# Attention and a SoLU layer on one core: low weight bits and lower halves moved to GpSimd, sums of squares to TensorE, larger units, another order

## The chip, the cores and the metric

The kernel runs on one core of one Trainium2 chip. A core has five engines that this kernel uses, each with a queue that it works through strictly in order: TensorE (PE: matrix products out of SBUF into PSUM), VectorE (DVE), ScalarE (ACT), GpSimd (POOL) and SyncE (SP), which only issues DMA transfers. Engines wait for each other by semaphores. The metric is the device time of one execution in microseconds (us).

## The reference

Attention with masks in 8 batches and 8 heads, then a SoLU layer (a product, a gate by softmax, a normalisation, a product). Cut to what is computed:

```python
# q, k, v: (8, 8, 576, 64) float32; w_in (512, 1024), w_out (1024, 512), g_ln (1024): float64
scores = np.matmul(q, k.transpose(0, 1, 3, 2)) / np.sqrt(64)
mask_local = (rel >= 0) & (rel < 32)                              # heads 0 to 3
mask_strided = (rel >= 0) & (pos[None, :] % 32 == pos[:, None] % 32)   # heads 4 to 7
attn = softmax(np.where(masks, scores, -1e9))
x = np.matmul(attn, v).transpose(0, 2, 1, 3).reshape(4608, 512)

h = x @ w_in
sm = softmax(h)
solu = h * sm
ln = (solu - mean(solu)) / np.sqrt(var(solu) + 1e-06) * g_ln
return (ln @ w_out).astype(np.float32)
```

## The kernel before, in words

**Plan and order.** The program is first written down as numbered steps: `add(engine, duration, function, reads, writes)`. A table of some 1,500 step numbers, `ORDER`, then says in which order the steps are issued, and with that the order in every engine's queue. The durations play no part in the order once the table is there. The semaphores follow from what each step reads and writes. So who stands behind whom is set by the table alone.

**Attention, in units.** Each batch has five units (`UNITS`): two for the strided heads (6 and 5 blocks of 54 queries) and three for the local heads (3 blocks each of 64 queries against 96 keys). One unit goes: score products of `q` and `k` into `s_ps` (L374), onto a mask seed that was written there before (for the first units by TensorE with a unit matrix, L369, from then on by ScalarE, L361); maximum of each row on VectorE (L380) and subtraction (L390) or, for some local units, the exponential block by block on ScalarE (L385); exponential (L392), row sum (L393), reciprocal (L397, L398), multiplication by it on GpSimd (L401); split of the probabilities into an upper half in float16 (ScalarE, L409) and a lower half (VectorE, L410); a transposing DMA (L412); product with `v` into `x_ps` (L432 strided, L442 local); split of `x` into halves (L461 ScalarE, L462 VectorE). `v` is scaled by a power of two that comes from the sum of its squares (L303 on ScalarE, L264, L270 and following) and split likewise (L325, L326).

**The SoLU layer, in 36 tiles of 128 tokens.** As soon as a batch's x is there, its tiles follow. FF1 (L505 to L507) is 24 products of 128x512: for each chunk upper by upper, upper by lower, lower by upper half. Then maximum (L511), exponential (ScalarE, L515), product with the exponential (VectorE, L517), mean and variance (L521, L522), some ten tiny steps on GpSimd (L525 to L555, for the first tiles L532 to L541), split of the normalised tile `cc` (L562 ScalarE, L563 VectorE), transposing DMA (L566), FF2 with `w_out` (L575 to L577, 24 products), output (L583).

**The weights.** They arrive as 64-bit numbers, 4 MB each in four pieces of 1 MB (`load`, L285, into `raw`, the last but one piece of w_out into `cc`). ScalarE makes a float32 of the upper word (`decode`, L603), VectorE shifts the lower word down (L606) and ORs three more bits in (L607). Then a power of two is found for a whole matrix from the sum of its squares: for w_in by TensorE (products of each block with itself, L620, of which VectorE reads the diagonal, L624), for w_out by ScalarE (L639, eight squares with an accumulator, joined with g squared on VectorE, L644 and L645). Then the matrix is split: w_in at L628 and L629, w_out, multiplied by g and the scale (`gs`, L649), at L651 (upper half, ScalarE) and L652 (lower half, VectorE). In the source:

```python
nc.vector.tensor_scalar(w0, w0, 29, None, op0=ALU.logical_shift_right)                       # L606
nc.vector.scalar_tensor_tensor(di, di, 3, w0, op0=ALU.logical_shift_left, op1=ALU.bitwise_or)  # L607
...
nc.vector.scalar_tensor_tensor(olo[:, cc], obuf[:, cc], gs_sb[:, cc : cc + 1], ohi[:, cc], op0=ALU.mult, op1=ALU.subtract)  # L652
```

Of the kernel before, what the change touches and what calls it, by code (L numbers as in the profile page):

```python
# [753 lines left out]
```

## Time and profile before

| what | value |
|---|---|
| three runs | 500.56, 502.09, 501.76 us (median 501.76) |
| profiled execution | 501.38 us, of it 499.7 us span from the first to the last instruction |
| mean granted TensorE clock | 0.952 |
| TensorE, products | 462.6 us busy (93% of the span) |
| VectorE / ScalarE / GpSimd | 352.0 / 363.3 / 159.8 us (70%, 73%, 32%) |
| DMA | 88.03 MB, mean 176 GB/s |

Line numbers (L505) are lines of the kernel before; names such as `h_ps<-w,xl` give output and inputs of an instruction. A bracket behind a row of the timeline, `[0.61 <-DVE raw L517]`, says how long the engine stood idle before it and what ended the wait. A matmul's 0.38 us contains its way through the pipeline; the next one starts earlier.

### The profile page before, as it was taken

The numbers are of one execution on the slowest core, as the hardware profiler recorded it, in microseconds if no ns is written. First come the engines' busy times: TensorE is split into PE (matmuls) and PEld (weight loads), VectorE is DVE, ScalarE is ACT, GpSimd is POOL, SyncE is SP. The second block draws the span as 40 slices with busy tenths as digits, with TensorE's granted clock in tenths as the row PEclk, the third lists the DMA queues.
The fourth block names the chain that finished last, engine by engine and source line by source line (L and its number), as shares of the span: only waits on it lengthen the run. The fifth ranks groups of instructions, "written<-read, shape, count | busy, mean of one in ns | idle before, by whom it ended". The sixth has DMA issues, their size and how long they took to land.

```text
span 499.7 us, 12461 instructions
## 1 busy us (share of the span) xinstructions
PE 462.6 (93%) x5049; PEld 241.4 (48%) x5049; DVE 352.0 (70%) x740; ACT 363.3 (73%) x647; POOL 159.8 (32%) x312
## 2 busy tenths in 40 slices
...
GB/s 330 336 326 261 353 187 163 158 189 184 187 207 180 133 259 257 131 173 231 213 145 197 254 185 175 84 90 218 85 138 121 78 123 101 132 102 74 84 97 106
DMA packets 153818, 88.03 MB, mean 176 GB/s; under 512 B 139808, under 2 KB 140448, under 8 KB 153248
## 3 DMA queue, kind: packets, MB, share of 16 engines
...
q8 instruction: 39, 0.64, 0.5%
q14 instruction: 19, 0.16, 0.1%
...
## 4 chain that ended last, share of the span: by engine, by line
PE 80%; DMA 13%; ACT 3%; SPq 2%; DVE 1%; issue 1%; ACTq 0%; DVEq 0%
PE h_ps L505 11%; PE o_ps L575 11%; PE h_ps L507 11%; PE h_ps L506 11%; PE o_ps L576 11%; PE o_ps L577 11%; PE s_ps L374 6%; DMA raw<-w_in 4%; DMA cc<-cc 3%; DMA raw<-w_out 3%; PE x_ps L442 3%; DMA pt<-p 3%; PE x_ps L432 2%; DMA q<-qstr 1%; ACT t L385 1%
## 5 line engine op out<-in xcount | busy, mean ns | idle before, releaser
L575 PE MATMUL o_ps<-ohi,cc 128*128 128x512 f16 x272 | 103.3, 380 | 0.2
L577 PE MATMUL o_ps<-ohi,cc 128*128 128x512 f16 x272 | 103.1, 379 | 0.0
L576 PE MATMUL o_ps<-obuf,cc 128*128 128x512 f16 x272 | 103.1, 379 | 0.0
L401 POOL TENSOR_TENSOR t<-t,m 128x576 f32<-128x576 f32 (+2 forms) x40 | 48.5, 1214 | 117.3 <-DVE m L398 93.8
L511 DVE TENSOR_REDUCE st<-h_ps 128x1 f32<-128x512 f32 x70 | 47.3, 681 | 32.6 <-PE h_ps L507 32.3
L563 DVE SCALAR_TENSOR_TENSOR cc<-raw,st,cc 128x1024 f16<-128x1024 f32 (+1 forms) x38 | 46.6, 1229 | 23.5 <-ACT cc L562 23.1
L515 ACT ACTIVATE raw<-h_ps,st,vsc 128x512 f32<-128x512 f32 x62 | 47.8, 773 | 19.7 <-DVE st L513 18.8
L505 PE MATMUL h_ps<-w,xl 128*128 128x512 f16 x140 | 53.7, 384 | 1.8 <-DVE raw L517 1.8
L517 DVE SCALAR_TENSOR_TENSOR raw<-h_ps,raw 128x512 f32<-128x512 f32 x70 | 47.1, 683 | 11.7 <-ACT raw L515 11.2
L374 PE MATMUL s_ps<-k,q 64*54 64x54 f32 (+1 forms) x1280 | 45.6, 284 | 9.1 <-ACT s_ps L361 7.4
L507 PE MATMUL h_ps<-w,xl 128*128 128x512 f16 x140 | 53.6, 383 | 0.0
L506 PE MATMUL h_ps<-w,xl 128*128 128x512 f16 x140 | 53.6, 383 | 0.0
L505 PE MATMUL h_ps<-w,xs 128*128 128x512 f16 x140 | 53.5, 382 | 0.0
L521 ACT ACTIVATE raw<-raw,st 128x1024 f32<-128x1024 f32 x36 | 41.3, 1147 | 16.8 <-DVE st L520 15.8
L506 PE MATMUL h_ps<-w,xs 128*128 128x512 f16 x140 | 53.3, 381 | 0.0
L507 PE MATMUL h_ps<-w,xs 128*128 128x512 f16 x140 | 53.3, 381 | 0.0
L562 ACT ACTIVATE cc<-raw,st 128x1024 f16<-128x1024 f32 (+1 forms) x38 | 41.5, 1100 | 13.9 <-POOL st L552 9.6
L374 PEld LDWEIGHTS s_ps<-k,q 64*54 64x54 f32 (+1 forms) x1280 | 40.0, 201 | 19.8 <-ACT s_ps L361 8.8
L380 DVE TENSOR_REDUCE m<-s_ps 128x6 f32<-128x576 f32 (+2 forms) x40 | 30.4, 760 | 25.7 <-PE s_ps L374 25.2
L577 PEld LDWEIGHTS <-cc 128*128 128x128 f16 x288 | 28.2, 98 | 34.5 <-DMA cc<-cc 0.6
L575 PEld LDWEIGHTS <-cc 128*128 128x128 f16 x288 | 28.1, 98 | 33.4 <-DMA cc<-cc 1.0
L576 PEld LDWEIGHTS <-cc 128*128 128x128 f16 x288 | 28.2, 98 | 31.5
...
## 6 DMA issues: line engine op xcount, KB each, us to landing
...
```

What stands on the lines that cost most here:

```text
L374: nc.tensor.matmul(s_ps[row : row + nq, pair, i * nk : (i + 1) * nk], q_raw[half][hs, q0 : q0 + (nq - 1) * nqb + 1 : nqb], k_raw[half][hs, ...
L401: add("pool", nx * nk / 520 + 0.03, lambda: nc.gpsimd.tensor_tensor(tv, tv, sm.unsqueeze(2).broadcast_to([P, nx, nk]), op=ALU.mult), r=TM, ...
L505: nc.tensor.matmul(hv[i], xhi[cc], whi[:, cc, cols], start=(cc == 0), stop=False)
L506: nc.tensor.matmul(hv[i], xhi[cc], wlo[:, cc, cols], start=False, stop=False)
L507: nc.tensor.matmul(hv[i], xlo[cc], whi[:, cc, cols], start=False, stop=(cc == 3))
L511: add("dve", 0.69, lambda i=i: nc.vector.tensor_reduce((nm, nm2)[i], hv[i], axis=AX.X, op=ALU.max, negate=True), r=[HH[i]], w=[(ST, "nm", i)])
L515: add("act", 0.73, lambda i=i, q=q: nc.scalar.activation(e[:, parts2[i]], hv[i], AF.Exp, bias=nm, scale=hs, accum_out=q), r=[HH[i], (ST, " ...
L517: add("dve", 0.7, lambda i=i, x=x: nc.vector.scalar_tensor_tensor(u[:, parts2[i]], hv[i], 1.0, e[:, parts2[i]], op0=ALU.mult, op1=ALU.mult ...
L563: add("dve", w / 980 + 0.23, lambda cols=cols: nc.vector.scalar_tensor_tensor(c[:, 1, cols], u[:, cols], r, c[:, 0, cols], op0=ALU.mult, o ...
L575: nc.tensor.matmul(o, ct[:, cc, :], ohi[:, cc, :], start=(cc == 0), stop=False)
L576: nc.tensor.matmul(o, ct[:, cc, :], olo[:, cc, :], start=False, stop=False)
L577: nc.tensor.matmul(o, ct[:, 8 + cc, :], ohi[:, cc, :], start=False, stop=(cc == 7))
```

## The change

1. *Units.* From batch 1 on the local heads go in units of 5 and 4 blocks (`LATER`) instead of three of 3; batch 0 keeps its five. The buffers `t`, `p` and `pt` have sizes of their own per kind of unit (four `p` buffers, three before). A unit of five blocks uses both banks of `x_ps`.
2. *Low bits.* The shift of the low word (L606 on VectorE) becomes one instruction on GpSimd that reads the top byte of the low word (L618 after). The OR on VectorE waits for it.
3. *Squares of w_out.* ScalarE's eight squares (L639) become 32 products on TensorE (L655 after) and one diagonal on VectorE (L659 after); the sum of the squares of g is multiplied in.
4. *Squares of v*, batches 0 and 1: ScalarE's squares (L303) become 22 products a batch (L310 after) and a diagonal (L313 after).
5. *Lower halves of w_out.* VectorE's one instruction (L652) becomes two on GpSimd, a multiplication (L667 after) and a subtraction (L668 after), eight times.
6. *Seeds.* All mask seeds are written by ScalarE; TensorE's seed products are gone. The opening products of TensorE are 12 of 128x480 instead of 40 of 128x128.
7. *Order.* `ORDER` is a new table. The loads begin with v and the first piece of w_in, then q and k.

What the new order does at three places. First VectorE round the first FF1, whose maximum is L511 (before) and L521 (after); `obuf` is w_out as it is decoded, `m` and `t` are a unit's maxima and scores. Before:

```order
L393 TENSOR_REDUCE m_89<-t_86 128x12
L397 TENSOR_SCALAR m_89<-m_89 128x12
L398 RECIPROCAL m_89<-m_89 128x12
L380 TENSOR_REDUCE m_90<-s_ps 128x10
L462 TENSOR_TENSOR xl_100<-x_ps,xl_99 128x2x192
L390 TENSOR_TENSOR t_87<-s_ps,m_90 128x540
L410 TENSOR_TENSOR p_95<-t_85,p_95 128x6x96
L606 TENSOR_SCALAR cc_103<-cc_103 128x1024
L607 SCALAR_TENSOR_TENSOR obuf_114<-obuf_114,cc_103 128x1024
L511 TENSOR_REDUCE st_106<-h_ps 128x1
L606 TENSOR_SCALAR raw_67<-raw_67 128x1024
```

After, up to the same maximum:

```order
L391 TENSOR_REDUCE m_88<-s_ps 128x10
L401 TENSOR_TENSOR t_84<-s_ps,m_88 128x540
L619 SCALAR_TENSOR_TENSOR obuf_113<-obuf_113,raw_67 128x1024
L640 SCALAR_TENSOR_TENSOR w_112<-cc_102,w_sc_114,w_112 128x1024
L421 TENSOR_TENSOR p_94<-t_85,p_94 128x6x96
L472 TENSOR_TENSOR xl_99<-x_ps,xl_98 128x2x192
L404 TENSOR_REDUCE m_87<-t_83 128x12
L391 TENSOR_REDUCE m_89<-s_ps 128x10
L619 SCALAR_TENSOR_TENSOR obuf_113<-obuf_113,cc_102 128x1024
L404 TENSOR_REDUCE m_88<-t_84 128x10
L398 TENSOR_SCALAR m_89<-m_89 128x10
L521 TENSOR_REDUCE st_105<-h_ps 128x1
```

The shifts (L606) are gone from between; the score blocks of batch 1 (`t_84<-s_ps`, `m_89<-s_ps`) stand ahead of the row sum of the unit before them (L404, before L393).

Second, GpSimd between the units of batch 1 and the small steps of the first tiles (`st_106` before and `st_105` after are tile 0). Before:

```order
L401 TENSOR_TENSOR t_86<-t_86,m_89 128x648
L401 TENSOR_TENSOR t_87<-t_87,m_90 128x540
L532 TENSOR_SCALAR st_106<-st_106 128x1
L533 TENSOR_TENSOR st_106<-st_106,nhalf_111 128x1
L401 TENSOR_TENSOR t_88<-t_88,m_91 128x576
L532 TENSOR_SCALAR st_107<-st_107 128x1
L533 TENSOR_TENSOR st_107<-st_107,nhalf_111 128x1
L525 TENSOR_SCALAR st_106<-st_106 128x1
```

After, in the same stretch:

```order
L412 TENSOR_TENSOR t_84<-t_84,m_88 128x540
L412 TENSOR_TENSOR t_85<-t_85,m_89 128x960
L667 TENSOR_SCALAR obuf_113<-obuf_113,gs_118 128x512
L668 TENSOR_TENSOR obuf_113<-obuf_113,ohi_109 128x512
L542 TENSOR_SCALAR st_105<-st_105 128x1
L543 TENSOR_TENSOR st_105<-st_105,nhalf_110 128x1
```

and, six more pairs of L667 and L668 further on:

```order
L667 TENSOR_SCALAR obuf_113<-obuf_113,gs_118 128x512
L668 TENSOR_TENSOR obuf_113<-obuf_113,ohi_109 128x512
L542 TENSOR_SCALAR st_106<-st_106 128x1
L543 TENSOR_TENSOR st_106<-st_106,nhalf_110 128x1
L535 TENSOR_SCALAR st_105<-st_105 128x1
L536 TENSOR_SCALAR st_105<-st_105,vsc_76 128x1
L537 TENSOR_SCALAR st_105<-st_105 128x1
```

Eight pairs now stand between the products of batch 1's units and the small steps of tile 1 (`st_106`), and one pair ahead of tile 0's.

Third, SyncE's loads round the second to fourth piece of w_out. Before:

```order
L285 DMA raw_67<-w_out 128x2x1024
L661 DMA g_118<-g 128x8
L412 DMA_TRANSPOSE pt_97<-p_96 128x12x128
L285 DMA cc_103<-w_out 128x2x1024
L285 DMA k_65<-kloc 128x1152
L285 DMA raw_67<-w_out 128x2x1024
L285 DMA q_63<-qloc 128x1152
L285 DMA vrs_70<-vstr 128x1536
```

After:

```order
L288 DMA raw_67<-w_out 128x2x1024
L288 DMA q_63<-qloc 128x1152
L288 DMA cc_102<-w_out 128x2x1024
L288 DMA raw_67<-w_out 128x2x1024
L288 DMA vrs_69<-vstr 128x1536
L423 DMA_TRANSPOSE pt_96<-p_94 128x12x128
L288 DMA raw_67<-vstr 128x1536
L288 DMA k_66<-kstr 128x1188
```

Batch 1's local q is now loaded behind w_out's second piece instead of the fourth, and the transposes of `p` stand elsewhere among the loads.

The diff, cut to its core (the whole table is new; two of its lines stand for it):

```diff
+LATER = [(1, 0, 6), (1, 6, 5), (0, 0, 5), (0, 5, 4)]
...
-1 5 7 2 0 6 8 11 10 13 12 15 14 17 9 21 3 25 4 29 53 45 54 55 68 56 46 57 69 47 58 70 59 48 71 49 88 60 72 83 73 61 51 74 89 62 90 84 18 91 52 22 100
+1 5 3 8 16 6 15 11 7 20 9 13 14 25 35 2 30 18 52 17 53 21 22 54 10 55 4 61 12 56 57 59 23 62 60 24 26 27 63 124 64 93 28 77 65 78 94 36 79 125 31 32
...
 def warm(n, out):
-    for _ in range(40):
-        nc.tensor.matmul(o_ps[:, 0:P], ones, ones, start=True, stop=True)
+    for i in range(n):
+        nc.tensor.matmul(out[i % len(out)], ones, ones[:, 0:1].broadcast_to([P, 5 * KL]), start=True, stop=True)
...
 def v_scale(b):
-            def square(a=a):
-                nc.scalar.activation(junk[:, 0 : VW[a]], vr_sb[raw][a], AF.Square, scale=2.0**-SQ, accum_out=vm[:, a : a + 1])
-            add("act", (1.36, 1.58)[a], square, r=[("vr", a, raw)], w=["junk", ("vm", b % 2, a)])
+        if b < 2:
+            for a in (1, 0):
+
+                def gram(a=a):
+                    x = vr_sb[raw][a].bitcast(BF16).rearrange("p (f t) -> p f t", t=2)[:, :, 1]
+                    for i in range(VW[a] // P):
+                        nc.tensor.matmul(h_ps[2][:, 0:P], x[:, i * P : i * P + P], x[:, i * P : i * P + P], start=(a == 1 and i == 0), stop=(a == 0 and i == VW[0] // P - 1))
+
+                add("pe", (0.75, 0.9)[a], gram, r=[("vr", a, raw)], w=[("h", 2)])
+            add("dve", 0.3, lambda: nc.vector.scalar_tensor_tensor(diag, h_ps[2][:, 0:P], 1.0, unit_sb, op0=ALU.mult, op1=ALU.mult, accum_out=vm[:, 0:1]),
+                r=[("h", 2), "unit"], w=[("vm", b % 2, a) for a in range(2)])
...
 def unit(n):
-    half, b0, nb = UNITS[j]
+    half, b0, nb = (LATER if b else UNITS)[j]
...
-        if n >= SEEDED:
-
-            def seed():
-                nc.scalar.copy(s_ps[:, :, 0 : nb * nk], mk.unsqueeze(1).broadcast_to([P, 2, nb * nk]))
-
-            add("act", nx * nk / 1200 + 0.17, seed, r=["mask"], w=[("s", 0), ("s", 1)])
+        add("act", nx * nk / 1200 + 0.17, lambda: nc.scalar.copy(sv, mk), r=[MK], w=[("s", 0), ("s", 1)])
...
-            for pair, h, hs, row in heads if n < SEEDED else ():
-                nc.tensor.matmul(s_ps[row : row + D, pair, 0 : nb * nk], unit_sb[hs, hs], mk[hs], start=True, stop=False)
...
 def decode(dst, src, n, w, room, shift=0):
-        def bits():
-            nc.vector.tensor_scalar(w0, w0, 29, None, op0=ALU.logical_shift_right)
-            nc.vector.scalar_tensor_tensor(di, di, 3, w0, op0=ALU.logical_shift_left, op1=ALU.bitwise_or)
-
-        add("dve", 2.02, bits, r=[*RAW, *w], w=[*w, *RAW], lock=True)
+        top = raw.bitcast(U8).rearrange("p f (t b) -> p f t b", b=4)[:, :, 0, 3]
+
+
+        add("pool", 1.05, lambda: nc.gpsimd.tensor_scalar(w0, top, -15.5, 1.0 / 32, op0=ALU.add, op1=ALU.mult), r=RAW, w=[("low", n)])
+        add("dve", 1.25, lambda: nc.vector.scalar_tensor_tensor(di, di, 3, w0, op0=ALU.logical_shift_left, op1=ALU.bitwise_or),
+            r=[*RAW, ("low", n), *w], w=[*w, *RAW], lock=True)
...
 def prep_o():
-            for cc in (2 * i, 2 * i + 1):
-                add("act", 0.71, lambda cc=cc: nc.scalar.activation(ob_sb[cc % 2][:, 0 : DM // 2].bitcast(BF16), obuf[:, cc], AF.Square,
-                                                                   scale=2.0**-SQ, accum_out=o_sc[:, 8 + cc : 9 + cc]),
-                    r=[("od", cc)], w=[("om", cc), ("ob", cc % 2)])
+            def gram(i=i, dst=dst):
+                x = dst.bitcast(BF16).rearrange("p (f t) -> p f t", t=2)[:, :, 1]
+                for j in range(8):
+                    nc.tensor.matmul(o_ps[:, 0:P], x[:, j * P : j * P + P], x[:, j * P : j * P + P], start=(i == 0 and j == 0), stop=(i == 3 and j == 7))
+
+            add("pe", 0.6, gram, r=OD, w=["o"])
+
+        add("dve", 0.3, lambda: nc.vector.scalar_tensor_tensor(diag, o_ps[:, 0:P], 1.0, unit_sb, op0=ALU.mult, op1=ALU.mult, accum_out=o_sc[:, 8:9]),
+            r=["o", "unit"], w=["om"])
...
-            add("dve", 0.74, lambda cc=cc: nc.vector.scalar_tensor_tensor(olo[:, cc], obuf[:, cc], gs_sb[:, cc : cc + 1], ohi[:, cc], op0=ALU.mult, op1=ALU.subtract),
-                r=["gs", ("oh", cc)], w=[("o_w", cc), ("od", cc)], lock=True)
+
+            def low(cc=cc):
+                nc.gpsimd.tensor_scalar(obuf[:, cc], obuf[:, cc], gs_sb[:, cc : cc + 1], None, op0=ALU.mult)
+                nc.gpsimd.tensor_tensor(olo[:, cc], obuf[:, cc], ohi[:, cc], op=ALU.subtract)
+
+            add("pool", 1.5, low, r=["gs", ("oh", cc)], w=[("o_w", cc), ("od", cc)])
```

More of the change, by code (lines that the diff above doesn't have):

```diff
@@ L160, in attn_solu_kernel @@
     (raw_sb,) = buf("raw", [P, 8, 1024], I32)
-    (junk,) = buf("junk", [P, 6 * 4 * D], BF16)
     VW = (NCL * 4 * D, 6 * 4 * D)
@@ L262, in total @@
             for i, part in enumerate(parts):
-                nc.tensor.matmul(tot, ones, part.bitcast(BF16)[:, 1:2], start=(i == 0 and not adds), stop=(i == len(parts) - 1), skip_group_check=adds)
+                one = product or not (i or adds)
+                nc.tensor.matmul(tot[:, i : i + 1] if product else tot, ones, part.bitcast(BF16)[:, 1:2], start=one, stop=product or i == len(parts) - 1, skip_group_check=adds)
         add("pe", 0.06 * len(parts) + 0.05, total, r=["ones", *r], w=[T])
         def root():
-            nc.vector.tensor_scalar(dst[:, 0:1].bitcast(I32), tot.bitcast(I32), 1, 0x7F800000, op0=ALU.logical_shift_right, op1=ALU.bitwise_and)
+            low = tot
+            if product:
+                low = dst[:, 0:1]
+                nc.vector.tensor_scalar(low, tot[:, 0:1], tot[:, 1:2], None, op0=ALU.mult)
+            nc.vector.tensor_scalar(dst[:, 0:1].bitcast(I32), low.bitcast(I32), 1, 0x7F800000, op0=ALU.logical_shift_right, op1=ALU.bitwise_and)
         def fn():
@@ L278, in fn @@
                 nc.vector.tensor_scalar(dst[:, 2:3], dst[:, 1:2], dst[:, 1:2], square, op0=ALU.mult, op1=ALU.mult)
-        add("dve", 0.16, root, r=[T], w=[(w, "root")])
+        add("dve", 0.32 if product else 0.16, root, r=[T], w=[(w, "root")])
         add("dve", 0.54, fn, r=[(w, "root")], w=[w])
@@ L300, in v_scale, with square @@
         raw = raw_v(b)
-        for a in range(2):
-            def square(a=a):
-                nc.scalar.activation(junk[:, 0 : VW[a]], vr_sb[raw][a], AF.Square, scale=2.0**-SQ, accum_out=vm[:, a : a + 1])
-            add("act", (1.36, 1.58)[a], square, r=[("vr", a, raw)], w=["junk", ("vm", b % 2, a)])
-        room = (s_ps[:, 1, 512 - b : 513 - b], ("s", 1)) if b else (h_ps[2][:, 0:1], ("h", 2))
-        pow2_scale(sc, [vm[:, 0:1], vm[:, 1:2]], [("vm", b % 2, a) for a in range(2)], ("vsc", b % 4), room, 8, 1.0 / P_SCALE, adds=b > 1)
+        if b < 2:
[7 more added lines that the diff above has]
+                r=[("h", 2), "unit"], w=[("vm", b % 2, a) for a in range(2)])
+            pow2_scale(sc, [vm[:, 0:1]], [("vm", b % 2, 0)], ("vsc", b % 4), (h_ps[2][:, 0:1], ("h", 2)), 8, 1.0 / P_SCALE, shift=0)
+        else:
+            junk = v_sb[1][b % 2]
+            for a in range(2):
+                def square(a=a):
+                    nc.scalar.activation(junk[:, a, 0 : VW[a]], vr_sb[raw][a], AF.Square, scale=2.0**-SQ, accum_out=vm[:, a : a + 1])
+                add("act", (1.36, 1.58)[a], square, r=[("vr", a, raw)], w=[("v", 1, b % 2, a), ("vm", b % 2, a)])
+            pow2_scale(sc, [vm[:, 0:1], vm[:, 1:2]], [("vm", b % 2, a) for a in range(2)], ("vsc", b % 4), (s_ps[:, 1, 512 - b : 513 - b], ("s", 1)), 8, 1.0 / P_SCALE, adds=True)
         def hscale():
@@ L404, in unit @@
         if half == 0:
-            hi, lo = (pb[:, 6 * a : 6 * a + 6, 0:nk] for a in range(2))
+            hi, lo = (pb[:, nx * a : nx * a + nx, 0:nk] for a in range(2))
         else:
@@ L449, in unit @@
             q0, w = off + QL * b0, QL * nb
-            src = [x_ps[xb][:, 0 : 2 * w].rearrange("p (c q) -> p c q", c=2)]
-            dst = [[x[:, :, q0 : q0 + w] for x in xl]]
+            src = [x_ps[xb][:, 0 : 2 * w].rearrange("p (c q) -> p c q", c=2)] if one else [x[:, 0:w] for x in x_ps]
+            dst = [[x[:, :, q0 : q0 + w] for x in xl]] if one else [[x[:, c, q0 : q0 + w] for x in xl] for c in range(2)]
             ring = [("xl", q0 // QL + i) for i in range(nb)]
```

101 lines of the change are left out of this document (51 added, 50 removed), and 81 rows, old and new, of the table ORDER.

## The prediction

> **What bounds the kernel now.** I read the busy shares by stage first, then what TensorE waits for, then the chain of work that ended last, then single rows. Stages: columns are start and end (us), length, then busy time of TensorE, its weight loads, VectorE, ScalarE and GpSimd (with counts), granted TensorE clock, DMA share, GB/s.
>
> ```profile
> 0.00:52.80 52.80, 24.28 (x553) 20.76 (x553) 39.25 (x75) 36.22 (x76) 10.45 (x22) 0.59 1.03 319
> 52.80:78.40 25.60, 21.52 (x275) 10.56 (x273) 21.53 (x47) 23.69 (x57) 5.03 (x5) 0.92 0.82 233
> 78.40:87.20 8.80, 8.79 (x60) 4.12 (x59) 8.16 (x18) 8.80 (x16) 1.06 (x3) 1.00 0.98 186
> 87.20:495.80 408.60, 407.77 (x4165) 205.94 (x4164) 283.07 (x603) 293.93 (x501) 143.28 (x283) 1.00 0.72 155
> ```
>
> From 87.2 us on TensorE is busy 407.77 of 408.60 us: there only TensorE's own work counts. Its one wait between 80 and 495 us, by the list of waits (us in total, times, longest):
>
> ```profile
> PE x_ps L442 <- DMA pt<-p: 0.5, 1, 0.5
> ```
>
> So the time is the start-up (87.2 us until the first FF2 ends) plus TensorE's work behind it plus a tail of 3.9 us. In the first 52.8 us VectorE is busy 39.25 us, GpSimd only 10.45, and the DMA engines all the time (share 1.03). Links of the chain of work that ended last (start, length, what):
>
> ```profile
> 6.66 18.86 DMA raw<-w_in
> ...
> 40.73 6.84 DMA raw<-w_out
> 47.60 1.19 ACT obuf L603
> 48.81 1.23 DVE obuf L607
> 50.07 7.03 DMA raw<-w_out
> ...
> 59.99 1.94 ACT ob L639 x6
> 61.93 0.77 ACT raw L515 x2
> 62.72 0.71 DVE raw L517 x2
> 63.47 0.38 PE h_ps L505
> ```
>
> This is what the change touches. FF1 of the first two tiles waits for loads of weights, for the decode that frees the buffer of the next load, and then for ScalarE, where six squares of w_out (1.94 us) stand ahead of the softmax exponential. TensorE there, by its timeline:
>
> ```profile
> 52.83 0.61 PE L505 MATMUL h_ps<-w,xl 128*128 128x512 f16 x1
> 63.47 0.38 PE L505 MATMUL h_ps<-w,xl 128*128 128x512 f16 x1 [0.61 <-DVE raw L517]
> 65.16 0.63 PE L507 MATMUL h_ps<-w,xl 128*128 128x512 f16 x1
> 65.59 0.63 PE L505 MATMUL h_ps<-w,xs 128*128 128x512 f16 x1
> 74.46 0.38 PE L505 MATMUL h_ps<-w,xl 128*128 128x512 f16 x1 [0.68 <-DVE raw L517]
> 78.41 0.38 PE L505 MATMUL h_ps<-w,xl 128*128 128x512 f16 x1 [0.52 <-DVE raw L517]
> 81.09 0.95 PE L374 MATMUL s_ps<-k,q 64*64 64x96 f32 x24
> 81.97 0.39 PE L575 MATMUL o_ps<-ohi,cc 128*128 128x512 f16 x1
> 86.94 0.38 PE L577 MATMUL o_ps<-ohi,cc 128*128 128x512 f16 x1
> ```
>
> Tile 0's FF1 starts at 52.83, tile 1's at 63.47, FF2 of tile 0 runs from 81.97 to 86.94 + 0.22 = 87.16. The 24 FF2 matmuls step by (86.94 - 81.97)/23 = 0.216 us; at 65.16 two stand 0.43 apart, and eight such steps between 63.9 and 67.3 lose 8 x 0.21 = 1.7 us; the granted clock of that stage is 0.92.
>
> **The change, part by part.** Prices come from these groups (line, forms, count | busy, mean ns | idle before):
>
> ```profile
> L606 DVE TENSOR_SCALAR raw<-raw 128x1024 int32<-128x1024 int32 x7 | 4.8, 691 | 1.4 <-DMA raw<-w_out 1.4
> L607 DVE SCALAR_TENSOR_TENSOR cc<-cc,raw 128x1024 int32<-128x1024 int32 x4 | 4.9, 1228 | 0.4
> L652 DVE SCALAR_TENSOR_TENSOR obuf<-obuf,gs,ohi 128x512 f16<-128x512 f32 x8 | 5.7, 746 | 0.2 <-ACT ohi L651 0.2
> L639 ACT ACTIVATE ob<-obuf 128x512 bf16<-128x512 f32 x8 | 5.0, 626 | 0.1
> L303 ACT ACTIVATE junk<-vrs 128x1536 bf16<-128x1536 f32 x5 | 7.4, 1477 | 0.0
> L303 ACT ACTIVATE junk<-vrl 128x1280 bf16<-128x1280 f32 x5 | 6.4, 1275 | 7.3 <-DMA vrl<-vloc 6.4 <-ACT ob L583 0.8
> L361 ACT CAST s_ps<-mk_loc 128x576 f32<-128x576 bf16 x21 | 13.5, 641 | 6.9 <-DVE t L390 4.0 <-ACT ob L583 0.8 <-DVE vsc L274 0.5
> L620 PE MATMUL h_ps<-cc 128*128 128x128 bf16 x32 | 4.1, 305 | 2.8 <-DVE cc L607 2.7
> L401 POOL TENSOR_TENSOR t<-t,m 128x576 f32<-128x576 f32 x24 | 28.4, 1183 | 70.3 <-DVE m L398 61.9 <-DVE vsc L316 4.3 <-ACT ob L583 4.0
> ```
>
> VectorE loses eight shifts of low bits (8 x 0.69 = 5.5 us) and eight lower halves (8 x 0.75 = 6.0), and gains three short diagonal reads (0.4 each). ScalarE loses eight squares of w_out (8 x 0.63 = 5.0) and v's first four (2 x (1.48 + 1.28) = 5.5), and gains six mask seeds (6 x 0.64 = 3.8), which took TensorE 24 matmuls. TensorE gains 32 products for w_out and 44 for v; by L620, 32 such take 4.1 us, at most, in a stage where it idles half the time. I cost them at nothing; their cover is the wait for loads.
>
> GpSimd gains all the rest, and its prices aren't in the trace. Nearest rows:
>
> ```profile
> 3.36 0.27 POOL L232 CAST mk_loc<-mask 128x96 bf16<-128x96 f32 x1
> 3.86 0.43 POOL L234 CAST mk_loc<-mask 128x288 bf16<-128x288 f32 x1
> 15.22 1.49 POOL L401 TENSOR_TENSOR t<-t,m 128x540 f32<-128x540 f32 x1 [1.18 <-DVE m L398]
> 62.83 1.09 POOL L401 TENSOR_TENSOR t<-t,m 128x540 f32<-128x540 f32 x1 [9.18 <-ACT raw L515]
> 72.47 1.77 POOL L533 TENSOR_TENSOR st<-st,nhalf 128x1 f32<-128x1 f32 x1
> ```
>
> The casts give 0.16 us for 192 more elements with one input: 0.19 + 0.00083 per element, so 0.61 for 512 and 1.04 for 1024. With two inputs, 576 take 1.18, so 512 take 1.05. A pair of the new lower half is 1.7 us, against 0.75 on VectorE; low bits 1.04 against 0.69. Upper end: the same 540-element product took 1.49 at 15.22 and 1.09 at 62.83, 1.37 times as long, so a pair costs up to 2.3. I take 1.7, by the 24 undisturbed rows. In all GpSimd gains 8 x (1.7 + 1.04) = 22 us in the first 88, where it was busy 10.45 + 5.03 + 1.06 = 16.5.
>
> The Trainium skill, "GPSIMD Engine Reference", section 3.1, states 2.6 cycles per element for two inputs and 1.03 for one, and section 4.1 advises VectorE for elementwise work, since GpSimd is about 2x slower with two inputs. By its 1.2 GHz a pair of 512 is an estimated 512 x 3.63/1.2 = 1.55 us before dispatch, and the sum would stay as by the rows. The 1.18 us of the 576-element row fits (2.6 cycles make 1.25).
>
> *First FF1.* Of VectorE's rows ahead of it, six shifts go (0.79 from start to start, 4.7 us) and a row sum with its reciprocal is put behind (1.1); two diagonals (0.7), a score subtraction of batch 1 (0.7) and a lower half of probabilities (0.7) come in: 3.7 us less. If VectorE decided, FF1 would start that much sooner. But the loads do: all four pieces of w_in and two of w_out must land first, with a DMA share of 1.03, and the new order puts batch 1's five-block score product ahead of FF1, whose local q is now loaded behind the second piece of w_out (before, behind the fourth). Walking the loads at 7 us a piece I get FF1 at 53.3, +0.4.
>
> *Second FF1.* The third piece of w_out waits for other buffers than before; the fourth lands about 57.5 (before 50.07 + 7.03 = 57.1). Its OR ends at 59.9; nine VectorE rows stand ahead of the diagonal (2.6 us); then exponential, the scale (two short products, five small steps) and gs at 65.9 (before 64.9). The six squares no longer delay the exponential, but the VectorE product that FF1 waits for stands behind the diagonal: FF1 of tile 1 at 64.7, +1.2.
>
> *To the end of the first FF2.* Before, 63.47 to 87.16 is 23.7 us: 84 matmuls (18.1), two strided products and one score product (2.5), waits for VectorE (0.68 + 0.52), 1.7 lost at the slow steps round 65 us. After, one strided product (0.8) comes behind FF2 and the score product has four blocks (+0.2): 23.1, so 87.8; 86.1 if the slow steps vanish. I take 87.6. GpSimd must have the lower halves by then. ScalarE's rows between gs and the last three upper halves (five such halves, two exponentials, two squares of v, a seed and others) sum to 12.2 us, and two waits for maxima add about 1.4, so the first of the three ends at 80.2; three pairs later, 80.2 + 5.1 = 85.3, the last lower half is there, and FF2 wants it at 82.6 + 22 x 0.216 = 87.3. No wait. But the row of tile 1 (up to 1.77 + 0.2 us) now stands behind these pairs on GpSimd's queue: 87.3, then ScalarE's upper half of tile 1 (1.15), then the seed of batch 2: 89.1, where TensorE asks for it at 87.6 + 0.8 = 88.4. About 0.8 us idle is new.
>
> *Behind it.* A score product of 24 holds TensorE for 81.97 - 81.09 = 0.88 us, one of 48 for 1.40:
>
> ```profile
> 102.03 1.46 PE L374 MATMUL s_ps<-k,q 64*54 64x54 f32 x48
> 103.43 0.39 PE L505 MATMUL h_ps<-w,xl 128*128 128x512 f16 x1
> ```
>
> So 0.022 us a matmul and 0.36 for each switch (another shape, so at most; by the local run's own step, (0.95 - 0.28)/23 = 0.029, it is 0.18). Three local units of 24 become 40 + 32, one switch less. Behind the first FF2 stood 19 of 24, 16.7 us; now come six batches of 40 + 32, 6 x (2.64 - 0.18 to 0.36) = 13.7 to 14.8. I take 14.1, which with the strided product put behind (+0.8) is -1.8. VectorE and ScalarE get fewer, longer instructions, hidden beside 0.69 and 0.72 busy.
>
> Sum against the profiled execution (501.38, span 499.7): +0.4 + 0.8 - 1.8 = -0.6, so 500.8. It lies 0.38 under the median of the runs, by which it would be 501.2; I say 500.9.
>
> **Rivals.** *The freed time counts (faster).* If loads follow VectorE rather than bound it (each w_out piece starts when a decode ends, as at 48.81 + 1.23 = 50.04 and 50.07), the 3.7 us of VectorE and the slow steps' 1.7 come off: 501 - 3 to 5, or 496 to 498.5. For it: VectorE is busy 39.25 of 52.8 us, and waits for its first score block at the start of them. Against: the share of 1.03.
>
> *The lower halves on GpSimd become the wait (slower).* It decides from a pair of (87.3 - 80.2)/3 = 2.37 us, the 2.3 of the disturbed row plus little. Beyond, FF2 of tile 0 waits piece by piece, and all small steps of tiles 0 and 1, which come behind in GpSimd's queue, wait too; at 2.9 us a pair FF2 ends 1.6 later, the second FF2's operand (5 us of transposes) 2 to 3 later, together +3 to +6: 504 to 507. For it: 1.49 against 1.09, while VectorE had an operation with two SBUF inputs. Against: the 24 of 576 elements above have a mean of 1.18. In the Trainium skill, "GPSIMD Engine Reference", section 8, GpSimd shares its SBUF interfaces with VectorE and contends with its instructions of two SBUF inputs; the pair of rows agrees.
>
> *The order doesn't do what it says* at batch 1's early score block: if local q lands late, FF1 of tile 0 starts at 55.3 and the time is 503; I hold it within the next paragraph's slower share.
>
> **How the numbers follow.** Likeliest, 0.38: 500.9, with its own range 499.5 to 502.5 (the slow steps' 1.7 us, the switch price, the idle). Faster, 0.33: 496 to 498.5. Slower, 0.29: 503.5 to 507. The range 496 to 506.5 leaves out under 2 in 10. About 0.3% (1.5 us) is what a measurement of this kernel can tell from no change; of the likeliest case 0.07 is faster by more, 0.28 within, 0.03 slower. Faster 0.40, same 0.28, slower 0.32.
>
> **What would show it.** FF1 of tile 0 within 1 us of 53.3 and DMA share about 1 before it: the loads bound; at 50 or less: the first rival. Pairs of 1.6 to 1.8 us on GpSimd and no wait in FF2 of tile 0: right; waits of FF2 for GpSimd over 1 us: the second rival. FF2 of tile 0 ending 87 to 88.5, a gap under 1.5 us before the next score product, and from there some 407 us of busy TensorE. It is wrong if TensorE shows waits beyond 100 us, or if the first 88 us move by more than 2 us.

## The result, and the profile after

The changed kernel takes 508.99 us (508.03 to 509.25), the kernel before, run beside it, 501.92: a ratio of 1.0147, 95% interval 1.0123 to 1.0171. The prediction said 500.9 in 496 to 506.5; it was wrong. The profiled execution spans 507.0 us, against 499.7. Line numbers are now those of the kernel after: L515 to L517 are FF1, L585 to L587 FF2, L385 the score product. The stages of the kernel after (start and end, length, busy time of TensorE, its weight loads, VectorE, ScalarE, GpSimd, granted clock, DMA share, GB/s):

```profile
0.00:53.08 53.08, 25.97 (x583) 20.56 (x584) 38.45 (x74) 35.08 (x73) 19.10 (x26) 0.67 0.99 326
53.08:78.20 25.12, 20.68 (x221) 10.74 (x217) 21.83 (x50) 22.10 (x50) 16.13 (x13) 0.95 0.97 267
78.20:92.70 14.50, 11.09 (x68) 4.87 (x68) 4.91 (x13) 7.88 (x26) 13.91 (x13) 0.88 0.76 176
92.70:503.10 410.40, 407.32 (x4199) 206.40 (x4198) 280.27 (x557) 289.22 (x460) 145.03 (x278) 1.00 0.69 149
```

Up to 53 us little has changed, but for GpSimd (19.10 us busy instead of 10.45). The first FF2 now ends at 92.67 instead of 87.16, and in the stage that holds it GpSimd is busy 13.91 of 14.50 us. What TensorE waits for from 80 us on (total us, times, longest):

```profile
PE o_ps L586 <- POOL obuf L668: 3.4, 3, 1.4
PE s_ps L385 <- ACT s_ps L376: 1.9, 2, 1.5
PE o_ps L585 <- DMA cc<-cc: 1.1, 1, 1.1
```

FF2's products with the lower half (L586) wait for GpSimd. TensorE's timeline there (start, length, what, idle before it):

```profile
64.22 0.38 PE L515 MATMUL h_ps<-w,xl 128*128 128x512 f16 x1 [1.43 <-DVE raw L527]
83.60 0.38 PE L585 MATMUL o_ps<-ohi,cc 128*128 128x512 f16 x1
86.68 0.38 PE L586 MATMUL o_ps<-obuf,cc 128*128 128x512 f16 x1 [1.41 <-POOL obuf L668]
89.46 0.38 PE L586 MATMUL o_ps<-obuf,cc 128*128 128x512 f16 x1 [0.68 <-POOL obuf L668]
92.24 0.38 PE L586 MATMUL o_ps<-obuf,cc 128*128 128x512 f16 x1 [1.32 <-POOL obuf L668]
94.97 1.47 PE L385 MATMUL s_ps<-k,q 64*54 64x54 f32 x48 [1.46 <-ACT s_ps L376]
97.31 0.63 PE L517 MATMUL h_ps<-w,xl 128*128 128x512 f16 x1
97.73 0.63 PE L515 MATMUL h_ps<-w,xl 128*128 128x512 f16 x1
```

The first FF1 (53.08, where the first stage ends) and the second (64.22) are where they were forecast. FF2 starts at 83.60 and takes 9.07 us instead of 5.19. Links of the chain of work that ended last (start, length, what): the first operation of one pair, then the last pair and what follows it:

```profile
78.28 1.55 POOL obuf L667
...
89.41 1.55 POOL obuf L667
...
91.04 1.15 POOL obuf L668
...
92.28 0.19 POOL st L542
...
92.55 0.59 POOL st L543
93.17 0.03 ACT cc L572
...
94.23 0.69 ACT s_ps L376
```

From 71.79 us pairs stand back to back on this chain (L667 multiplies by the scale, L668 subtracts the upper half). A pair takes 89.41 - 78.28 = 11.13 us for four, 2.78 each, where 1.7 was forecast. Behind the last pair come tile 1's small steps (L542, L543), ScalarE's L572, the seed L376, and only then the score product at 94.97.

The account of the +7.3 us of span: the end of the first FF2 is 5.5 us later (start +1.6, its own length +3.9). Behind it 414.3 us remain, 1.8 more than before's 412.5: the idle of 1.46 ahead of the score product, 1.1 for the transposed activations, and eight steps between 96.5 and 100 at 0.43 us instead of 0.216, 1.7 us, together 4.3. Without these 410.0 remain (a further wait of 0.4 us for a seed is still in them), against 412.0 before without its wait of 0.5.

### The profile page after: what moved, and what is told of

It reads as the page before. It is cut to its first block, busy times and chain, and to the rows that moved or that the text cites. A ratio compares the mean times of both kernels' runs of the same rounds, so it can differ in the third digit from the quotient of the medians.

```text
span 507.0 us, 12397 instructions
## 1 busy us (share of the span) xinstructions
PE 465.3 (92%) x5065; PEld 242.6 (48%) x5065; DVE 345.5 (68%) x691; ACT 355.0 (70%) x609; POOL 194.2 (38%) x328
## 4 chain that ended last, share of the span: by engine, by line
PE 68%; ACT 9%; POOL 8%; DMA 6%; DVE 5%; issue 3%; ACTq 0%; POOLq 0%; DVEq 0%; SPq 0%
PE o_ps L585 10%; PE o_ps L586 10%; PE o_ps L587 9%; PE h_ps L515 9%; PE h_ps L516 9%; PE h_ps L517 9%; PE s_ps L385 5%; DMA raw<-w_in 3%; POOL obuf L667 3%; PE x_ps L452 2%; POOL obuf L668 2%; DMA cc<-cc 1%; ACT t L396 1%; PE x_ps L442 1%; POOL t L412 1%
## 5 line engine op out<-in xcount | busy, mean ns | idle before, releaser
L586 PE MATMUL o_ps<-obuf,cc 128*128 128x512 f16 x272 | 103.1, 379 | 3.4 <-POOL obuf L668 3.4
L585 PE MATMUL o_ps<-ohi,cc 128*128 128x512 f16 x272 | 103.2, 379 | 1.1 <-DMA cc<-cc 1.1
L587 PE MATMUL o_ps<-ohi,cc 128*128 128x512 f16 x272 | 103.1, 379 | 0.0
L521 DVE TENSOR_REDUCE st<-h_ps 128x1 f32<-128x512 f32 x70 | 47.2, 683 | 41.8 <-PE h_ps L517 41.4
L412 POOL TENSOR_TENSOR t<-t,m 128x648 f32<-128x648 f32 (+4 forms) x33 | 46.9, 1426 | 60.2 <-DVE m L409 52.8
L573 DVE SCALAR_TENSOR_TENSOR cc<-raw,st,cc 128x1024 f16<-128x1024 f32 (+1 forms) x38 | 48.5, 1277 | 27.0 <-ACT cc L572 27.0
L385 PE MATMUL s_ps<-k,q 64*54 64x54 f32 (+1 forms) x1280 | 44.0, 285 | 24.3 <-ACT s_ps L376 16.1
L572 ACT ACTIVATE cc<-raw,st 128x1024 f16<-128x1024 f32 (+1 forms) x38 | 41.7, 1103 | 28.5 <-POOL st L562 20.5
L515 PE MATMUL h_ps<-w,xl 128*128 128x512 f16 x140 | 54.6, 390 | 2.7 <-DVE raw L527 2.7
L516 PE MATMUL h_ps<-w,xl 128*128 128x512 f16 x140 | 54.6, 390 | 0.0
L517 PE MATMUL h_ps<-w,xl 128*128 128x512 f16 x140 | 54.5, 389 | 0.0
L385 PEld LDWEIGHTS s_ps<-k,q 64*54 64x54 f32 (+1 forms) x1280 | 38.8, 201 | 31.6 <-ACT s_ps L376 22.4
L515 PE MATMUL h_ps<-w,xs 128*128 128x512 f16 x140 | 53.6, 383 | 0.0
L517 PE MATMUL h_ps<-w,xs 128*128 128x512 f16 x140 | 53.2, 380 | 0.0
L535 POOL TENSOR_SCALAR st<-st 128x1 f32<-128x1 f32 x36 | 13.5, 374 | 92.1 <-ACT raw L525 90.4
L587 PEld LDWEIGHTS <-cc 128*128 128x128 f16 x288 | 28.2, 98 | 37.9 <-issue 4.3
L593 ACT ACTIVATE ob<-o_ps,st 128x512 f32<-128x512 f32 x34 | 23.3, 684 | 31.4 <-PE o_ps L587 20.6
L560 POOL TENSOR_SCALAR st<-st 128x1 f32<-128x1 f32 x32 | 7.1, 222 | 98.1 <-ACT raw L532 97.3
```

The costliest lines, as they stand in the source:

```text
L385: nc.tensor.matmul(s_ps[row : row + nq, pair, i * nk : (i + 1) * nk], q_raw[half][hs, q0 : q0 + (nq - 1) * nqb + 1 : nqb], k_raw[half][hs, ...
L412: add("pool", nx * nk / 520 + 0.03, lambda: nc.gpsimd.tensor_tensor(tv, tv, sm.unsqueeze(2).broadcast_to([P, nx, nk]), op=ALU.mult), r=TM, ...
L515: nc.tensor.matmul(hv[i], xhi[cc], whi[:, cc, cols], start=(cc == 0), stop=False)
L516: nc.tensor.matmul(hv[i], xhi[cc], wlo[:, cc, cols], start=False, stop=False)
L517: nc.tensor.matmul(hv[i], xlo[cc], whi[:, cc, cols], start=False, stop=(cc == 3))
L521: add("dve", 0.69, lambda i=i: nc.vector.tensor_reduce((nm, nm2)[i], hv[i], axis=AX.X, op=ALU.max, negate=True), r=[HH[i]], w=[(ST, "nm", i)])
```

## The experiments

Two theories of the loss: the lower halves on GpSimd (A), or the new order with its units of 5 and 4 (B). Then, inside A: is it the multiplication's form, its factor, or where it stands?

**The lower halves back on VectorE** (the rest of the change stays):

```diff
...
-                nc.gpsimd.tensor_scalar(obuf[:, cc], obuf[:, cc], gs_sb[:, cc : cc + 1], None, op0=ALU.mult)
-                nc.gpsimd.tensor_tensor(olo[:, cc], obuf[:, cc], ohi[:, cc], op=ALU.subtract)
...
+            add("dve", 0.74, lambda cc=cc: nc.vector.scalar_tensor_tensor(olo[:, cc], obuf[:, cc], gs_sb[:, cc : cc + 1], ohi[:, cc], op0=ALU.mult, op1=ALU.subtract),
...
```

> The changed kernel with one part undone: the eight lower halves of w_out are again one VectorE instruction each (0.75 us), at the same places of the same order. Theory A (the pairs on GpSimd, 1.56 + 1.16 us, are the whole loss): TensorE waits for no lower half, the first FF2 ends near 87.5 us instead of 92.7, the 1.46 us wait for the seed of batch 2 and the 1.7 us of slow steps behind it go too, and the time is 500.5 to 502, level with before or a little faster. Rival B (the new order, its loads and units cost something of their own): 504 or more, with waits left in the first 100 us.

Measured 500.83 us, ratio 1.0008 (0.9998 to 1.0018). TensorE's waits from 50 to 495 us hold none for GpSimd:

```profile
PE s_ps L385 <- ACT s_ps L376: 2.9, 4, 1.4
PE x_ps L452 <- DMA pt<-p: 2.1, 1, 2.1
PE h_ps L515 <- DVE raw L527: 1.8, 2, 1.1
PE o_ps L585 <- DMA cc<-cc: 0.2, 1, 0.2
```

So the whole loss is in the lower halves, and all the other parts together come to nothing that the times show (0.1 us faster to 0.9 slower). In this execution the first FF2 ends at 88.2, 1.0 later than before, and behind it 410.7 us remain instead of 412.5.

**The multiplication with two tensor operands** (the factor broadcast):

```diff
-                nc.gpsimd.tensor_scalar(obuf[:, cc], obuf[:, cc], gs_sb[:, cc : cc + 1], None, op0=ALU.mult)
+                nc.gpsimd.tensor_tensor(obuf[:, cc], obuf[:, cc], gs_sb[:, cc : cc + 1].broadcast_to([P, DM]), op=ALU.mult)
```

> The changed kernel with the multiplication of the pair written as a product of two tensors (the per-partition factor repeated along the row) instead of a product with a per-partition factor. Theory C (the factor read from memory makes that form slow, 3 ns an element): the multiplication takes about 1.05 to 1.15 us like other two-input products of 512 on GpSimd, a pair 2.3 instead of 2.75, the last lower half comes 3.5 us sooner, and the time is 504 to 506. Rival D (VectorE's traffic or the float32 write in place slows it): the multiplication stays at 1.5 or more and the time at 508 to 510.

Measured 506.22, ratio 1.0112 (1.0093 to 1.0131). The groups of instructions (count | busy, mean ns):

```profile
L668 POOL TENSOR_TENSOR obuf<-obuf,ohi 128x512 f16<-128x512 f32 x8 | 10.5, 1308 | 0.6
L667 POOL TENSOR_TENSOR obuf<-obuf,gs 128x512 f32<-128x512 f32 x8 | 9.3, 1162 | 3.0 <-ACT ohi L664 3.0
```

A multiplication of two tensors takes 1.16 us in the mean and 1.04 undisturbed (without the instructions that the last section shows stretched), less than the 1.57 by a scalar. Undisturbed pairs start 2.23 to 2.24 us apart, and FF2 waits 2.2 us for GpSimd instead of 3.4. GpSimd's last two multiplications:

```profile
85.57 1.04 POOL L667 TENSOR_TENSOR obuf<-obuf,gs 128x512 f32<-128x512 f32 x1
87.81 1.04 POOL L667 TENSOR_TENSOR obuf<-obuf,gs 128x512 f32<-128x512 f32 x1
```

The price is as theory C had it, the time just above its range.

**A constant factor** (0.5 instead of the scale in memory):

```diff
-                nc.gpsimd.tensor_scalar(obuf[:, cc], obuf[:, cc], gs_sb[:, cc : cc + 1], None, op0=ALU.mult)
+                nc.gpsimd.tensor_scalar(obuf[:, cc], obuf[:, cc], 0.5, None, op0=ALU.mult)
```

> The changed kernel with a constant (0.5) in place of the per-partition factor in that multiplication, so the lower halves have wrong values and only the time counts. Theory C: 0.6 to 0.7 us for 512 elements, as the casts of before priced it, a pair 1.8, no wait of FF2 for GpSimd, and 500.5 to 502.5. Rival D: it stays near 1.5 us and the time near 509.

Measured 509.07, ratio 1.0166 (1.0149 to 1.0183). Theory C falls: that the factor is read from memory is not the cause.

```profile
L667 POOL TENSOR_SCALAR obuf<-obuf 128x512 f32<-128x512 f32 x8 | 12.9, 1608 | 3.0 <-ACT ohi L664 3.0
```

Undisturbed it takes 1.49 to 1.51 us, 0.06 less than with the factor from memory.

**The kernel before, with only the pairs on GpSimd** (the same two instructions in the old order):

```diff
-            add("dve", 0.74, lambda cc=cc: nc.vector.scalar_tensor_tensor(olo[:, cc], obuf[:, cc], gs_sb[:, cc : cc + 1], ohi[:, cc], op0=ALU.mult, op1=ALU.subtract),
...
+                nc.gpsimd.tensor_scalar(obuf[:, cc], obuf[:, cc], gs_sb[:, cc : cc + 1], None, op0=ALU.mult)
+                nc.gpsimd.tensor_tensor(olo[:, cc], obuf[:, cc], ohi[:, cc], op=ALU.subtract)
```

> The kernel before with this one part of the change alone: the eight lower halves as pairs on GpSimd, in the old order. Theory A: eight pairs of 2.75 us from about 67 us on, with the old order's products and small steps between them, end near 92 us; the first FF2 waits for them and ends 4 to 6 us later than 87.2; time 506 to 510. Rival B: under 504.

Measured 511.07, ratio 1.0213 (1.0197 to 1.0229), above even the 506 to 510 of theory A. Its wait, from the list of waits:

```profile
PE o_ps L576 <- POOL obuf L654: 8.8, 3, 4.8
```

The new order doesn't cause the loss; it softens it.

**Eight forms of the operation**, one for each row block (the lower halves come out other than the reference's):

```diff
+                if cc == 0:
+                    nc.gpsimd.tensor_scalar(x, x, gcc, None, op0=ALU.mult)
+                elif cc == 1:
+                    nc.gpsimd.tensor_scalar(x, x, 1.0, 0.5, op0=ALU.add, op1=ALU.mult)
+                elif cc == 2:
+                    nc.gpsimd.tensor_scalar(x, x, 1.0, None, op0=ALU.add)
...
```

> The changed kernel with eight different first instructions in the eight pairs, to price the form (values wrong, only the rows' durations count): the factor from memory in place on 512 (as it was), a constant sum times a constant in place, a constant sum alone, the product into another buffer of 256, a product into float16, a plain copy of 256, the product in place on 256, the product of float16 input into float16. Theory F (float32 through this arithmetic form costs 3 ns an element whatever the factor is): all float32 forms with one input take about 1.5 for 512 and 0.85 for 256, the copy about 0.4. Rival G (writing over its own input costs it): the product into another buffer takes 0.4 to 0.5 for 256 and the one in place 0.85. Rival H (only a single operation is slow): the sum times a constant takes about 0.6 to 0.8, the others 1.5.

Run once, for the durations alone. From the groups, in order: two operations, one addition of a constant, into another buffer as f16, f16 to f16, 256 columns in place, a copy of 256:

```profile
L674 POOL TENSOR_SCALAR obuf<-obuf 128x512 f32<-128x512 f32 x1 | 0.6, 617 | 0.0
L676 POOL TENSOR_SCALAR obuf<-obuf 128x512 f32<-128x512 f32 x1 | 1.5, 1512 | 0.0
L680 POOL TENSOR_SCALAR spare<-obuf,gs 128x512 f16<-128x512 f32 x1 | 1.6, 1563 | 0.0
L686 POOL TENSOR_SCALAR spare<-ohi,gs 128x512 f16<-128x512 f16 x1 | 1.6, 1570 | 0.0
L684 POOL TENSOR_SCALAR obuf<-obuf,gs 128x256 f32<-128x256 f32 x1 | 0.9, 932 | 3.0 <-ACT ohi L667 3.0
L682 POOL COPY spare<-obuf 128x256 f32<-128x256 f32 x1 | 0.4, 396 | 0.0
```

A block of the same size in the same buffer, written in place, takes 617 ns with two operations and 1512 with one. Type and target make next to no difference (1512 to 1570), and the form with a single operation is the slow one, as rival H had it. The form of the kernel after was stretched in this run (2.19 us). The size does scale it: 932 for 256. Each form ran once here, at its own moment; the next run puts the two forms in the same place, eight times each.

**The change with a second operation that does nothing**, a multiplication by 1:

```diff
-                nc.gpsimd.tensor_scalar(obuf[:, cc], obuf[:, cc], gs_sb[:, cc : cc + 1], None, op0=ALU.mult)
+                nc.gpsimd.tensor_scalar(obuf[:, cc], obuf[:, cc], gs_sb[:, cc : cc + 1], 1.0, op0=ALU.mult, op1=ALU.mult)
```

> The changed kernel with one word more: the multiplication of the pair carries a second operation, times 1.0, which leaves its values as they were. Theory H (GpSimd's product with a factor is slow only as a single operation, 3.0 ns an element, and fast with two, 1.2): it takes 0.62 us, a pair 1.8 as the prediction had it, TensorE waits for no lower half, the first FF2 ends by 88 us, and the time is 499.5 to 501, 8 us below the changed kernel and level with before or just below. Rival M (the short time belonged to the constant factors): 1.5 us and 509.

Measured 502.82, ratio 1.0038 (1.0024 to 1.0052). The groups, and TensorE's row behind the first FF2:

```profile
L668 POOL TENSOR_TENSOR obuf<-obuf,ohi 128x512 f16<-128x512 f32 x8 | 10.4, 1302 | 0.7
L667 POOL TENSOR_SCALAR obuf<-obuf,gs 128x512 f32<-128x512 f32 x8 | 6.1, 767 | 3.4 <-ACT ohi L664 3.4
```

```profile
89.64 1.48 PE L385 MATMUL s_ps<-k,q 64*54 64x54 f32 x48 [1.35 <-ACT s_ps L376]
91.43 0.63 PE L516 MATMUL h_ps<-w,xl 128*128 128x512 f16 x1
91.86 0.63 PE L517 MATMUL h_ps<-w,xl 128*128 128x512 f16 x1
```

The multiplication takes 0.69 us undisturbed, FF2 no longer waits for GpSimd (its last product starts at 87.14), and of the 1.5% lost 0.4% is left. The mechanism is theory H's; the time is above the 499.5 to 501 that it expected. What is left shows in the three rows: an idle of 1.35 us, which the prediction had named (as 0.8), and slow steps behind it (0.43 us apart).

**The same, with the last lower half on VectorE**, so that tile 1's small steps come one pair sooner on GpSimd:

```diff
+            if cc == 7:
+                add("dve", 0.74, lambda cc=cc: nc.vector.scalar_tensor_tensor(olo[:, cc], obuf[:, cc], gs_sb[:, cc : cc + 1], ohi[:, cc], op0=ALU.mult, op1=ALU.subtract),
+                    r=["gs", ("oh", cc)], w=[("o_w", cc), ("od", cc)], lock=True)
```

> The kernel after with the two-operation multiplication, and the last of the eight lower halves (row block 7) computed by VectorE in one instruction instead of the pair on GpSimd. Everything else as in the kernel after. Theory Q (what is left of the loss with the two-operation form, 502.8 against 501, is the idle of TensorE at 89.6 us, because the small steps of tile 1 at L542 and L543 stand behind the last pair on GpSimd, then ScalarE's L572, then the seed of the score product): with the last pair gone GpSimd reaches L542 at about 84.9 instead of 87.0, ScalarE's L572 starts when its copies end at 86.3 instead of 87.84, the seed ends about 1.5 us sooner, and the idle of 1.35 us ahead of the 64x54x48 score product falls to 0.0 to 0.3. Time 500.7 to 501.8. VectorE has 2.9 us free between 83.4 and 86.3, where the new instruction of about 0.75 us falls. Rival R (the idle is only shifted: another wait takes its place, for the transposed activations or for the seed): the wait of about 1 us appears at one of the next products and the time stays at 502.3 to 503.3.

Measured 501.10, ratio 1.0003 (0.9987 to 1.0019). TensorE's rows, the last product of the first FF2 and what follows:

```profile
88.50 0.38 PE L587 MATMUL o_ps<-ohi,cc 128*128 128x512 f16 x1
...
89.38 1.46 PE L385 MATMUL s_ps<-k,q 64*54 64x54 f32 x48
...
90.90 0.38 PE L515 MATMUL h_ps<-w,xl 128*128 128x512 f16 x1
91.11 0.38 PE L516 MATMUL h_ps<-w,xl 128*128 128x512 f16 x1
```

The idle is gone, and so are the slow steps behind it. GpSimd reached L542 only at 86.58 instead of the expected 84.9, because the whole stage came some 1.5 us later in this execution, where twelve slow steps stand at the second FF1, between 65.2 and 70.3 us; the kernel above has none there. But the order of events is what was expected, and the time is in theory Q's range. Behind the first FF2 remain 500.0 - 88.72 = 411.3 us, against 501.5 - 87.36 = 414.1 in the kernel above. The intervals of the two ratios don't meet.

**The kernel before, with two-operation pairs on GpSimd.** The edit differs from that of the old order above in one line:

```diff
-                nc.gpsimd.tensor_scalar(obuf[:, cc], obuf[:, cc], gs_sb[:, cc : cc + 1], None, op0=ALU.mult)
+                nc.gpsimd.tensor_scalar(obuf[:, cc], obuf[:, cc], gs_sb[:, cc : cc + 1], 1.0, op0=ALU.mult, op1=ALU.mult)
```

> The kernel before with the lower halves alone on GpSimd, the multiplication with the second operation. Theory H: pairs of 1.8 us, 14.4 in all instead of 22.6; the old order's last lower half comes some 8 us sooner than with single operations (there the first FF2 waited 8.8 us), so 1 to 2 us of wait are left at most: 500.5 to 503. Rival N (any pass of the lower halves over GpSimd holds the old order up, whatever its price): 506 or more.

Measured 506.3, ratio 1.0111 (1.0092 to 1.0131): outside theory H's range, and at rival N's 506. The old order starts the second pair only at 74.03, and the last one ends at 88.65. TensorE's list of waits:

```profile
PE o_ps L576 <- POOL obuf L654: 4.2, 2, 3.0
```

So the new order is needed for the cheap pair to be hidden.

**What sets the first FF1.** Four edits on the kernel with the lower halves on VectorE, or with the two-operation pairs. First the OR on 8 columns instead of 1024 (the part of the line that changes):

```diff
...
-nc.vector.scalar_tensor_tensor(di, di, 3, w0, op0=ALU.logical_shift_left, op1=ALU.bitwise_or)
+nc.vector.scalar_tensor_tensor(di[:, 0:8], di[:, 0:8], 3, w0[:, 0:8], op0=ALU.logical_shift_left, op1=ALU.bitwise_or)
...
```

> The variant with the lower halves on VectorE, and the OR of the low bits on 8 columns only (the last bits of most weights are left out): VectorE has 8 x 1.1 us less, 6 of these ahead of tile 0's first FF1. Theory I (the loads set the start of FF1): it starts within 1.5 us of 53.0, and the time is 499 to 501. Rival J (VectorE sets it): it starts at 46 to 49, and the time is 494 to 498.

Measured 500.88, ratio 0.9997 (0.9970 to 1.0024). Stages of the kernel with the OR, then of this one:

```profile
0.00:53.00 53.00, 28.13 (x584) 22.06 (x585) 38.37 (x74) 34.95 (x73) 18.91 (x26) 0.62 1.00 326
```

```profile
0.00:53.17 53.17, 27.55 (x583) 21.74 (x584) 33.71 (x75) 35.10 (x73) 16.81 (x26) 0.65 1.03 332
```

VectorE is busy 4.7 us less and FF1 starts no sooner, as theory I expected. Its chain up to FF1 runs over the load of local q, then mostly over ScalarE:

```profile
7.43 16.43 DMA q<-qloc
...
26.43 2.05 ACT t L396 x12
...
37.08 2.04 ACT t L396 x12
39.12 1.04 ACT w L639
```

Then, from 43.11 to 48.55, it stands in a stretch that the chain doesn't name, in front of the low bits of w_out's second piece. GpSimd's row names the load:

```profile
48.60 1.14 POOL L618 TENSOR_SCALAR raw<-raw 128x1024 int32<-128x1024 uint8 x1 [5.49 <-DMA raw<-w_out]
```

Second, the low bits back on VectorE:

```diff
-        add("pool", 1.05, lambda: nc.gpsimd.tensor_scalar(w0, top, -15.5, 1.0 / 32, op0=ALU.add, op1=ALU.mult), r=RAW, w=[("low", n)])
+        add("dve", 0.7, lambda: nc.vector.tensor_scalar(w0, w0, 29, None, op0=ALU.logical_shift_right), r=RAW, w=[("low", n)])
```

> The variant with the lower halves on VectorE, and the low bits shifted down by VectorE again (8 x 0.69 us), in the same order. Theory I (freed VectorE time ahead of FF1 is worth nothing, the loads set its start): within 1 us of the variant, 500 to 502. Rival J: 3 to 5 us slower, 504 to 506.

Measured 502.29, ratio 1.0019 (1.0004 to 1.0034). FF1 starts at 54.63 and 66.45, 1.5 to 1.6 us later than with the low bits on GpSimd, though the two ratios' intervals overlap. By the time it is theory I's (0.5 us slower by the ratios), but VectorE's work there isn't wholly free: FF1 did move, and the chain of work that ended last runs mostly over VectorE from 43 to 56 us here.

Third, some 25 steps of the order moved, so that FF1 of tile 1 comes sooner. On ScalarE's queue, for instance, the two reads of tile 0's FF1 go ahead of a softmax's ten rows:

```diff
 ACTIVATE obuf<-raw 128x1024
+ACTIVATE raw,st<-h_ps,st,vsc 128x512 x2
 ACTIVATE t,m<-s_ps,m 128x96 x10
-ACTIVATE raw,st<-h_ps,st,vsc 128x512
 CAST p<-t 128x12x54
-ACTIVATE raw,st<-h_ps,st,vsc 128x512
-ACTIVATE vl<-vrl,vsc 128x1280
-CAST xl<-x_ps 128x2x192
```

> The variant with the lower halves on VectorE and some 25 steps round 58 to 70 us in another order: the maxima and exponentials of tile 0 ahead of the block-by-block exponentials of batch 1's five-block unit on ScalarE, w_out's diagonal behind the first product of tile 0 on VectorE, and the last product with v of batch 0 behind the first half of tile 1's FF1 on TensorE instead of ahead of the sum for the scale. Theory K (what is left of the start-up is who stands behind whom): tile 1's FF1 starts at 62 to 63 instead of 64.9, the first FF2 ends 1.5 to 2.5 us sooner, time 498 to 499.5, below before. Rival L (the waits come back elsewhere, at transposes or at the seeds): within 0.3% of the variant.

Measured 504.53, ratio 1.0073 (1.0051 to 1.0094). FF1 came at 63.57, sooner than the variant's 64.94, and a longer wait came back behind it, so the time is worse than both theories had it:

```profile
76.97 0.59 PE L522 MATMUL h_ps<-w,xl 128*128 128x512 f16 x1 [4.62 <-DVE raw L534]
```

Fourth, the two-operation kernel with batch 0's local k and q loaded ahead of the last two pieces of w_in. SyncE's queue:

```diff
-DMA raw_67<-w_in 128x2048 x3
+DMA raw_67<-w_in 128x2048
 DMA k_65<-kloc 128x1152
 DMA q_63<-qloc 128x1152
+DMA raw_67<-w_in 128x2048 x2
```

> The variant with the second operation, and batch 0's local k and q loaded behind the second piece of w_in instead of the fourth, with the steps that wait for them moved forward on ScalarE, VectorE and GpSimd and the decode of the last two pieces behind them. Theory O (up to 24 us the chain waits for loads, then ScalarE's exponentials block by block follow each other): the first local score block starts at 20 to 22 instead of 23.9 us, tile 0's FF1 1 to 3 us sooner, time 497.5 to 500. Rival P (what is gained there is given back at w_in's last pieces or at w_out's loads): within 0.3% of the variant.

Measured 503.89, ratio 1.0056 (1.0042 to 1.0069): no gain. The first local score block came 1.3 us sooner, but from the third one on they came 1.4 us later, and so did tile 0's FF1; FF1 of tile 1 started at 65.90 instead of 64.88. The time is as rival P had it. None of the orders tried brings the start-up forward as a whole.

## Why the prediction was wrong, point by point

- *The price of the pair* is the step that failed. The multiplication was priced at 0.61 us from casts, rows of another operation. It took 1.57, the subtraction 1.16 (forecast 1.05), the pair 2.78 instead of 1.7. With the two-operation form, 0.69 us undisturbed, the pair is near the forecast (0.69 + 1.16), and the result, 502.82, lies in the range; 500.9 was 1.9 too low even then.
- *The threshold* of 2.37 us a pair was too high. With two tensor operands the pairs behind the last upper halves start 2.23 us apart (2.47 us is the mean with the stretched ones), and FF2 waits 2.2 us. With two operations they start 1.91 us apart, and it is just enough: the last lower half is there at 86.88 (85.72 + 1.16), and the product that wants it starts at 86.93. So the limit lies near 1.9 us (an estimate from these two runs), inside the range that the prediction gave for a pair, up to 2.3. That range took its upper end from a stretched row of a two-input product and held no row of the operation itself.
- *The slower rival* (504 to 507, chance 0.29) is what happened, at its place and by its mechanism, but its price was too low. It counted three pairs, behind the last three upper halves, the first of which it had at 80.2. They came sooner: ScalarE's row of the three runs from 78.08 to 80.02. But GpSimd had a backlog: five pairs, from 78.28, ended at 92.19. This count is also what put the threshold too high. So FF2 ended 5.1 us later than the forecast 87.6, not 1.6. And slow steps followed the idle, 1.7 us, which weren't in the price.
- *The first FF1* at 53.3: 53.08. *The second* at 64.7: 64.22. *Low bits* at 1.04 us: 1.12. All right. The reason given for the first, that the loads decide, was half right: time freed on VectorE beyond this change is worth nothing there, as forecast against the first rival (496 to 498.5, which fell), but the chain runs over ScalarE too, and with the low bits back on VectorE FF1 comes 1.6 us later.
- *The new idle* of 0.8 us ahead of batch 2's score product, by tile 1's small steps behind the pairs on GpSimd: 1.35 us with the cheap pairs, and gone when one pair is taken away. Right in mechanism, too small, and its slow steps were left out; by the times (502.82 to 501.10) it cost 1.7 us.
- *The stage behind* at -1.8 us: 410.7 (lower halves on VectorE) and 411.3 us, with waits of 0.2 and 1.0 in them, against 412.5 with 0.5, so -1.5 to -1.7, by one execution of each. Right.

The sum of all the parts, -0.6 us, isn't borne out either. Without the pairs on GpSimd the new idle of 0.8 us falls away, so the same working gives -1.4 us; by the times it is +0.4 us (-0.1 to +0.9). The first FF2 came 0.6 us later than forecast in that execution; the rest isn't accounted for. Of the 1.5% lost, about 1.1% is the one-operation form, and 0.35% goes with the last pair, behind which the small steps queue. No version tried is faster than the kernel before by more than the measurement can tell.
